# A fused attention and gated-MLP kernel: TensorE's order written out from a clock, head sums over four slices, softmax and weight broadcast in halves

## The chip, the cores and the metric

The kernel runs on one core of one Trainium2 chip, in one launch. The metric is the device time of an execution in microseconds (us). Three runs of the kernel before took 763.28, 763.34 and 765.01 us; their median is 763.34 us.

## The reference

One token sequence of 2048 rows with 1024 features goes through two pre-norm blocks in bf16. The first is a local attention with 32 heads of 32 features. Each position attends to 8 positions, itself and those 2, 4, ... 14 rows back:

```python
qkv = (x @ wqkv).reshape(B, S, 3, H, Dh).transpose(2, 0, 3, 1, 4)
idx = pos[:, None] - (jnp.arange(8) * 2)[None, :]
logits = einsum('bhsd,bhswd->bhsw', q, k[idx]) * Dh ** -0.5     # masked where idx < 0
o = einsum('bhsw,bhswd->bhsd', softmax(logits), v[idx])
h = x + (o heads joined) @ wo                                    # x is layer-normed for wqkv
```

The second is a gated MLP on the layer norm of h. `z = gelu(hn @ w_in)` has 3584 columns. The first half is z1; the second is layer-normed to z2, mixed over the positions (`g = w_sp @ z2 + b_sp`), and the output is `h + (z1 * g) @ w_out`.

## The kernel before, in words

The sequence is cut into four chunks c = 0..3 of 512 rows. The dense work on TensorE (PE) for a chunk is: `qkv(c)` (L225, 192 matmuls of 512 columns), the attention's output projection, called the head, H0 to H3 (`b_head`, L343, 64 matmuls at L358), `b_z2(c)` (L399, 128 matmuls at L415, half of the groups with 256-column tails) and `b_z1(c)` (L439, 112 matmuls at L447). When all chunks are through, the spatial mix (L523) and the output projection (L540) follow; they run with little else beside them.

Each group of 16 matmuls fills one accumulator (`new_acc`, L107), a PSUM tile of two banks out of a ring of three. ScalarE (ACT) empties it: a copy `stg` for qkv (L256), a gelu for z2 and z1 (L417, L450). VectorE (DVE) empties the head's (L369). A fourth pair of banks, tag "L", holds first the logits and then, one after the other, the four tiles `pb` of broadcast weights.

The attention of a chunk (`attention`, L263) is DVE's work with short helpings from PE and ACT. For each of 8 offsets DVE multiplies q and shifted k (L278, 128x4096), adds the upper half of the slices to the lower (L280, 128x2048) and once more (L281, 128x1024). After four offsets PE sums over the features of a head with a 0/1 matrix E32: 8 matmuls with 32 output rows each (L285), placed in four column groups. Then comes the softmax: maximum (L290), subtract (L292), exp on ACT (L296), sum (L298), reciprocal (L300), scale (L302). PE spreads each head's weights over its four partitions (L311) and ACT copies them to AB (L314). Eight products with v and seven additions (L320 to L324) give oT, which the head reads. DVE does the offsets of the next chunk directly after.

Around the head: DVE adds the residual (L369), ACT squares it for the statistics (L371), small DVE steps and one GpSimd (POOL) power give rstd (`batch_rstd`, L327 to L339; the last small step is l2nb at L338), ACT normalizes (`hnc`, L384), and a transposing DMA on SP's queue (L385) makes hnT, the input of z2 and z1. For z2 the chain is the same: ACT squares (L426), the small steps end in l3nb, and DVE normalizes four tiles of 128x1792 (L435). In the last chunk the transposes are made on PE (`head_fin`, L388).

The order on each engine is set by a scheduler from the order of the calls at L461 to L501, from buffer rings and from `tc.high_priority()` blocks; each engine then works strictly in its order and waits where an input or a buffer isn't ready. SP's queue issues most DMAs in order, POOL's queue the loads of q, k, v and of the weights.

Of the kernel before, what the change touches and what calls it, by code (L numbers as in the profile page):

```python
# [10 lines left out]
FP32 = mybir.dt.float32  # L11
BF16 = mybir.dt.bfloat16
# [22 lines left out]
XRB = 2  # L35
# [18 lines left out]
def kernel(  # L54
# [76 lines left out]

    warm = l1.tile([P, CH], BF16, name="warm", tag="xn", bufs=4)
# [91 lines left out]

    def qkv(c):  # L225
# [4 lines left out]
        if c >= 1:  # L230
            xnT[c] = xtp.tile([P, KT, CH], BF16, name="xnT", tag="xnT")
            nc.sync.dma_start_transpose(xnT[c][:], xn_d[c].rearrange("s (a p) -> s a p", p=P))
        for xi in range(3):
            wv = wsb[xi][:].rearrange("p kt (m dl) -> p kt dl m", dl=DLO)
            for dp in range(DLO // 2):
                if c == 0 and xi == 0 and dp < 2:
                    if dp == 0:
                        accs = [new_acc(), new_acc()]
                        for kt in range(KT):
                            for dl in range(4):  # L240
                                T.matmul(accs[dl // 2][:, dl % 2, :], wv[:, kt, dl, :], xnT[c][:, kt, :],  # L241
                                         start=(kt == 0), stop=(kt == KT - 1))
                    acc = accs[dp]
                else:
                    acc = new_acc()
                    for j in range(2):
                        dl = 2 * dp + j
                        for kt in range(KT):
                            T.matmul(acc[:, j, :], wv[:, kt, dl, :], xnT[c][:, kt, :],  # L249
                                     start=(kt == 0), stop=(kt == KT - 1))  # L250
                if c == 0:
                    off = 0 if xi == 0 else HALO
                    A.copy(tiles[xi][:, 2 * dp:2 * dp + 2, off:off + CH], acc[:])  # L253
                else:
                    stg = l1.tile([P, 2, CH], BF16, name="stg", tag="xn", bufs=4)
                    A.copy(stg[:], acc[:])  # L256
                    dma(qkv_d[xi][:, 2 * dp:2 * dp + 2, c * CH:(c + 1) * CH], stg[:])
            if c == 0 and xi > 0:
# [4 lines left out]
    def attention(c):  # L263
        if c == 0:
            qT, kT, vT = att_in[0]
        else:
            qT, kT, vT = alloc_att_in(c)
# [3 lines left out]

        L = ps_att.tile([P, W_WIN, P], FP32, name="L", tag="L")
        for w4 in range(2):
            part = att.tile([P, 4, 2, CH], BF16, name=f"part{w4}", tag="sc8" if w4 == 0 else "part")
            for wi in range(4):
                o = HALO - DIL * (4 * w4 + wi)
                prod = att.tile([P, DLO, CH], BF16, name="prod", tag="prod")
                V.tensor_tensor(prod[:], qT[:], kT[:, :, o:o + CH], op=ALU.mult)  # L278
                t1_ = att.tile([P, 4, CH], BF16, name="t1", tag="t1")
                V.tensor_tensor(t1_[:], prod[:, 0:4, :], prod[:, 4:8, :], op=ALU.add)  # L280
                V.tensor_tensor(part[:, wi], t1_[:, 0:2, :], t1_[:, 2:4, :], op=ALU.add)  # L281
            with tc.high_priority():
                for z in range(2):
                    for sq in range(4):
                        T.matmul(L[32 * sq:32 * sq + 32, 4 * w4:4 * w4 + 4, :], E32, part[:, :, z, sq * P:(sq + 1) * P],  # L285
                                 start=(z == 0), stop=(z == 1), tile_position=(0, 32 * sq))
        if c == 0:
            V.tensor_tensor(L[0:32, :, 0:16], L[0:32, :, 0:16], maskb, op=ALU.add)
        m = att.tile([P, P], FP32, name="mx", tag="mx")
        V.tensor_reduce(m[:], L[:].rearrange("p w s -> p s w"), axis=AX.X, op=ALU.max)  # L290
        Ls = att.tile([P, W_WIN, P], FP32, name="Ls", tag="t1")
        V.tensor_tensor(Ls[:], L[:], m[:].unsqueeze(1).to_broadcast([P, W_WIN, P]), op=ALU.subtract)  # L292
        e_t = att.tile([P, W_WIN, P], BF16, name="e", tag="prod")
        e = e_t[:]
        with tc.high_priority():
            A.activation(e, Ls[:], ACTF.Exp, scale=SCALE)  # L296
        ssum = att.tile([P, P], FP32, name="ssum", tag="ssum")
        V.tensor_reduce(ssum[:], e.rearrange("p w s -> p s w"), axis=AX.X, op=ALU.add)  # L298
        rinv = att.tile([P, P], FP32, name="rinv", tag="rinv")
        V.reciprocal(rinv[:], ssum[:])  # L300
        attn = att.tile([P, W_WIN, P], BF16, name="attn", tag="attn")
        V.tensor_tensor(attn[:], e, rinv[:].unsqueeze(1).to_broadcast([P, W_WIN, P]), op=ALU.mult)  # L302

        AB = att.tile([P, W_WIN, CH], BF16, name="AB", tag="sc8")
        with tc.high_priority():
            for w4 in range(2):
                for sh in range(2):
                    pb = ps_att.tile([P, 2, 4, P], FP32, name="pb", tag="L")
                    for j in range(2):
                        sq = 2 * sh + j  # L310
                        T.matmul(pb[:, j], B4[32 * sq:32 * sq + 32, :],  # L311
                                 attn[32 * sq:32 * sq + 32, 4 * w4:4 * w4 + 4, :],
                                 start=True, stop=True, tile_position=(32 * sq, 0))
                    A.copy(AB[:, 4 * w4:4 * w4 + 4, sh * 256:(sh + 1) * 256].rearrange("p w (j s) -> p j w s", j=2), pb[:])  # L314
        oT = att.tile([P, DLO, CH], BF16, name="oT", tag="oT", bufs=OTB)
        for w in range(W_WIN):
# [4 lines left out]
            else:  # L321
                prod = att.tile([P, DLO, CH], BF16, name="prod", tag="prod")
                V.tensor_tensor(prod[:], vT[:, :, o:o + CH], abb, op=ALU.mult)  # L323
                V.tensor_tensor(oT[:], oT[:], prod[:], op=ALU.add)  # L324
        oTs[c] = oT

    def batch_rstd(sums, sqs, n, pfx):  # L327
# [10 lines left out]
        V.scalar_tensor_tensor(nb[:], mean[:], -1.0, rstd[:], op0=ALU.mult, op1=ALU.mult)  # L338
        return mean, rstd, nb  # L339

    hnTs = {}

    def b_head(c):  # L343
        oT = oTs[c]
        hsum = bp.tile([P, TPC], FP32, name="hsum", tag="hsum")
# [3 lines left out]
        mvl = bp.tile([P, TPC, 2], FP32, name="mvl", tag="mvl", bufs=1)  # L349
        for il in range(TPC):  # L350
# [3 lines left out]
            last = (c == NCH - 1)  # L354
            acc = new_acc()
            for dl in range(DLO):
                for nh in range(2):
                    T.matmul(acc[:, nh, :], oT[:, dl, il * P:(il + 1) * P], wo_sb[:, dl, nh * CH:(nh + 1) * CH],  # L358
                             start=(dl == 0), stop=(dl == DLO - 1))
            accf = acc[:].rearrange("p a b -> p (a b)")  # L360
            hb = bp.tile([P, D], BF16, name="hb", tag="hb", bufs=TPC)
            if last:
                V.tensor_tensor(hb[:], accf, xr[:], op=ALU.add)
                st = bp.tile([P, 2, 6], FP32, name="bnst2", tag="bnst2")
                V.bn_stats(st[:, 0, :], hb[:, 0:512])
                V.bn_stats(st[:, 1, :], hb[:, 512:1024])
                V.bn_aggr(mvl[:, il, :], st[:])
            else:
                V.scalar_tensor_tensor(hb[:], accf, 1.0, xr[:], op0=ALU.mult, op1=ALU.add,  # L369
                                       accum_out=hsum[:, il:il + 1])  # L370
                A.activation(hnc[:, il, :], hb[:], ACTF.Square, accum_out=hsq[:, il:il + 1])  # L371
            dma(h_d[i * P:(i + 1) * P, :], hb[:])
            hbs.append(hb)
        hnT = bp.tile([P, TPC, KT, P], BF16, name="hnT", tag="hnT")
        hnTs[c] = hnT
        if c == NCH - 1:
# [4 lines left out]
            return lambda: head_fin(hnT, hnc, hbs, mvl[:, :, 0], rstdl)  # L381
        mean2, rstd2, nb2 = batch_rstd(hsum[:], hsq[:], D, "l2")
# [5 lines left out]
    def head_fin(hnT, hnc, hbs, mean2, rstd2):  # L388
        for il in range(TPC):
            V.tensor_scalar(hnc[:, il, :], hbs[il][:], mean2[:, il:il + 1], rstd2[:, il:il + 1],  # L390
                            op0=ALU.subtract, op1=ALU.mult)
            tp = ps_tp2.tile([P, KT, P], BF16, name="tp2", tag="tp2")
            for a in range(KT):
                T.transpose(tp[:, a, :], hnc[:, il, a * P:(a + 1) * P], ident)
            V.tensor_copy(hnT[:, il], tp[:])

    z2sb = {}

    def b_z2(c):  # L399
        hnT = hnTs[c]  # L400
# [4 lines left out]
        for il in range(TPC):  # L405
            u = l1.tile([P, FH], BF16, name="u", tag="x4k", bufs=4)
            for hf in range(2):
# [4 lines left out]
                for kt in range(KT):  # L412
                    for n0 in range(0, wd, CH):
                        n1 = min(n0 + CH, wd)
                        T.matmul(accf[:, n0:n1], hnT[:, il, kt, :], wt[:, kt, n0:n1],  # L415
                                 start=(kt == 0), stop=(kt == KT - 1))
                A.activation(u[:, hf * 1024:hf * 1024 + wd], accf[:, 0:wd], ACTF.Gelu_apprx_tanh,  # L417
                             accum_out=sums[:, il, hf:hf + 1])
            if c < NCH - 1:
# [11 lines left out]
        mean3, rstd3, _ = batch_rstd(stot[:], sqs[:], FH, "l3")  # L431
        for il in range(TPC):
            i = c * TPC + il
            z2 = z2t[il]
            V.tensor_scalar(z2[:], us[il][:], mean3[:, il:il + 1], rstd3[:, il:il + 1], op0=ALU.subtract, op1=ALU.mult)  # L435
# [3 lines left out]
    def b_z1(c, lo=0, hi=NF // 2):  # L439
        hnT = hnTs[c]  # L440
        for fp in range(lo, hi):
            acc = new_acc()
            for j in range(2):
                f = 2 * fp + j
                wt, f0 = (wins[2], f) if f < 8 else (wins[3], f - 8)
                for kt in range(KT):
                    T.matmul(acc[:, j, :].rearrange("p (a b) -> p a b", a=TPC), wt[:, kt, f0 * P:(f0 + 1) * P], hnT[:, :, kt, :],  # L447
                             start=(kt == 0), stop=(kt == KT - 1))
            z1s = l1.tile([P, 2, CH], BF16, name="z1s", tag="xn", bufs=4)
            A.activation(z1s[:], acc[:], ACTF.Gelu_apprx_tanh)  # L450
            st = dma(z1_d[2 * fp:2 * fp + 2, :, c * CH:(c + 1) * CH].rearrange("f p s -> p f s"), z1s[:])
        return st
# [7 lines left out]

    qkv(0)  # L461
    qkv(1)
    attention(0)
    qkv(2)
    b_head(0)
    attention(1)
    qkv(3)
# [3 lines left out]
    b_head(1)  # L471
    t1.close()
    t2 = ExitStack()
    bq = t2.enter_context(tc.tile_pool(name="bq", bufs=2))

    for c in range(NCH):
        b_z2(c)
        if c == 0:
            load_win(3, bq.tile([P, KT, 768], BF16, name="win3", bufs=1))
        Z1SPLIT = {1: 0, 2: 3}.get(c, 0)  # L480
        if Z1SPLIT:
            b_z1(c, 0, Z1SPLIT)
        if 0 < c and c + 1 < NCH:
            fin = b_head(c + 1)
        if c + 1 == NCH - 1:
# [7 lines left out]
            ps_tp2 = ctx.enter_context(tc.tile_pool(name="ps_tp2", bufs=2, space=PSUM))  # L493
            fin()
        last_store = b_z1(c, Z1SPLIT)
        if c + 1 == NCH - 1:
            tc.add_manual_dep(wsp0_inst.ins, last_store.ins.name,
                              mybir.DependencyInfo(mybir.DependencyClass.NoSync, mybir.DependencyReason.DATA),
                              reason="keep the xbar transpose out of the z1 store stream")
        if c + 2 < NCH:  # L500
            attention(c + 2)  # L501
# [80 lines left out]
```

## Time and profile before

| what | value |
|---|---|
| median of three runs | 763.34 us |
| the profiled execution's own time | 764.78 us |
| its span, first to last instruction | 763.0 us |
| PE busy | 737.8 us (97%) |
| DVE busy | 440.9 us (58%) |
| ACT busy | 200.0 us (26%) |
| mean granted TensorE clock | 0.987 |
| first spatial matmul (L523) | 468.3 us after the span's start |

How to read it: a profile row has the start and duration in us, engine, line, operation, the tile written and the tiles read. The bracket at its end is the idle time of that engine just before it and who ended it. PE's busy share says little, since a matmul's record lasts about 0.38 us while one starts every 0.216 us; what counts is the distance between starts. Until 468 us, PE's dense work, DVE's attention and ACT's copies go on side by side and wait for each other; after it PE runs 0.216 us per matmul to the end. The change lies entirely in the part before 468 us.

### The profile page before, as it was taken

What the parts mean: (1) busy time and instruction counts of PE and PEld (TensorE: products, weight loads), DVE (VectorE), ACT (ScalarE), POOL (GpSimd) and SP (SyncE); (2) the same over time, 40 slices, a digit from 0 to 9 for tenths busy, and PEclk for the clock granted to TensorE, in tenths of its full rate; (3) what the DMA queues carried; (4) which work ended last, traced back from release to release, by engine and by line L of the source; (5) the groups of instructions that cost most, each with busy time, mean ns of one, the idle gap of its engine ahead of it and who ended that gap; (6) DMA issues with size and microseconds to landing.
All of it is one profiled execution on the core that took longest, in us unless ns stands there. A gap on an engine that the chain in (4) does not pass through costs nothing.

```text
span 763.0 us, 8382 instructions
## 1 busy us (share of the span) xinstructions
PE 737.8 (97%) x3502; PEld 369.5 (48%) x3502; DVE 440.9 (58%) x431; ACT 200.0 (26%) x250; POOL 32.3 (4%) x40
## 2 busy tenths in 40 slices
PE   7999999899998999899989999999999999999997
PEld 3666566455544445344534544444444444444443
DVE  4889799998989799997985010332233122222322
ACT  3332532236318736347611542000000000000000
POOL 0000000010101100000004010000000000000000
PEclk8999999999999999999999999999999999999999
DMA  9994464165893541334057869416211711020001
GB/s 337 335 239 116 142 164 140 55 218 172 233 324 92 172 146 57 125 125 111 0 182 286 209 226 220 161 42 179 70 34 39 191 55 41 28 83 27 1 24 60
DMA packets 109623, 104.20 MB, mean 137 GB/s; under 512 B 63537, under 2 KB 87377, under 8 KB 109457
## 3 DMA queue, kind: packets, MB, share of 16 engines
q1 hardware_dynamic: 103120, 76.89, 33.9%
q0 software_dynamic: 6176, 26.26, 10.1%
q8 instruction: 27, 0.44, 0.3%
q10 hardware_dynamic: 288, 0.52, 0.2%
q14 instruction: 12, 0.09, 0.0%
HBM read 55.09 MB, written 33.88 MB: 117 GB/s over the span
## 4 chain that ended last, share of the span: by engine, by line
PE 60%; DVE 29%; issue 8%; POOL 1%; ACT 1%; DMA 0%; POOLq 0%; DVEq 0%; ACTq 0%
PE acc L523 25%; PE acc L540 12%; DVE oT L324 7%; DVE prod L323 7%; PE acc L249 7%; PE acc L447 6%; DVE prod L278 6%; PE acc L415 3%; PE acc L358 3%; PE acc L241 1%; DVE hb L369 1%; DVE oT L320 1%; PE acc L548 1%; DVE u L435 1%; DMA xp<-in_A_x_dram 0%
## 5 line engine op out<-in xcount | busy, mean ns | idle before, releaser
L278 DVE TENSOR_TENSOR prod<-qT,kT 128x4096 bf16<-128x4096 bf16 x32 | 73.2, 2286 | 2.3 <-ACT kT L253 2.2
L415 PEld LDWEIGHTS <-hnT 128*128 128x128 bf16 x512 | 50.0, 99 | 48.9 <-issue 3.9
L540 PEld LDWEIGHTS <-zg 128*128 128x128 bf16 x420 | 41.1, 98 | 49.5
L323 DVE TENSOR_TENSOR prod<-vT,AB 128x4096 bf16<-128x4096 bf16 x28 | 64.2, 2291 | 1.0
L324 DVE TENSOR_TENSOR oT<-oT,prod 128x4096 bf16<-128x4096 bf16 x28 | 64.2, 2292 | 0.9
L358 PE MATMUL acc<-wo_sb,oT 128*128 128x512 bf16 x256 | 57.6, 387 | 4.8 <-DVE oT L324 4.8
L415 PE MATMUL acc<-win_1620,hnT 128*128 128x512 bf16 x256 | 60.2, 387 | 0.0
L542 DVE TENSOR_TENSOR ot<-acc,hr 128x1024 bf16<-128x1024 f32 x15 | 18.4, 1225 | 69.4 <-PE acc L540 69.4
L249 PE MATMUL acc<-xnT,wv 128*128 128x512 bf16 x256 | 58.3, 386 | 0.0
L447 PE MATMUL acc<-hnT,win_1624 128*128 128x512 bf16 x256 | 58.0, 384 | 0.0
L256 ACT CAST stg<-acc 128x1024 bf16<-128x1024 f32 x36 | 36.2, 1012 | 80.7 <-PE acc L249 70.0
L249 PE MATMUL acc<-xnT,wk 128*128 128x512 bf16 x256 | 56.1, 379 | 0.0
L540 PE MATMUL acc<-wout_a,zg 128*128 128x512 bf16 x240 | 54.2, 379 | 0.0
L249 PE MATMUL acc<-xnT,wq 128*128 128x512 bf16 x224 | 50.3, 381 | 0.0
L450 ACT ACTIVATE z1s<-acc 128x1024 bf16<-128x1024 f32 x28 | 28.6, 1023 | 70.6 <-PE acc L447 69.4
L249 PEld LDWEIGHTS <-wv 128*128 128x128 bf16 x256 | 36.6, 145 | 20.5 <-issue 3.2
L249 PEld LDWEIGHTS <-wk 128*128 128x128 bf16 x256 | 36.8, 144 | 18.7 <-issue 0.4
L415 PE MATMUL acc<-win_1622,hnT 128*128 128x512 bf16 (+1 forms) x256 | 44.4, 326 | 0.0
L358 PEld LDWEIGHTS <-oT 128*128 128x128 bf16 x256 | 25.3, 100 | 36.6 <-DVE oT L324 5.8
L447 PE MATMUL acc<-hnT,win_1922 128*128 128x512 bf16 x192 | 42.8, 379 | 0.0
L540 PE MATMUL acc<-wout_b,zg 128*128 128x512 bf16 x180 | 41.3, 379 | 0.0
L249 PEld LDWEIGHTS <-wq 128*128 128x128 bf16 x224 | 31.8, 145 | 17.0 <-issue 1.8
(358 smaller groups left out, 937.8 us busy)
## 6 DMA issues: line engine op xcount, KB each, us to landing
z_d<-z1s SPq DMA_DIRECT2D x28, 256.0 KB, 2.5
z1c<-z_d SPq DMA_DIRECT2D x28, 256.0 KB, 2.8
z_d<-u SPq DMA_DIRECT2D x12, 448.0 KB, 3.2
xr<-in_A_x_dram SPq DMA_DIRECT2D x16, 256.0 KB, 3.5
h_d<-hb SPq DMA_DIRECT2D x16, 256.0 KB, 3.0
hr<-h_d SPq DMA_DIRECT2D x16, 256.0 KB, 2.8
out_dram<-ot SPq DMA_DIRECT2D x15, 256.0 KB, 2.1
xp<-in_A_x_dram SPq DMA_DIRECT2D x14, 256.0 KB, 10.1
```

Source lines behind the costliest of these rows:

```text
L249: T.matmul(acc[:, j, :], wv[:, kt, dl, :], xnT[c][:, kt, :], start=(kt == 0), stop=(kt == KT - 1))
L256: A.copy(stg[:], acc[:])
L278: V.tensor_tensor(prod[:], qT[:], kT[:, :, o:o + CH], op=ALU.mult)
L323: V.tensor_tensor(prod[:], vT[:, :, o:o + CH], abb, op=ALU.mult)
L324: V.tensor_tensor(oT[:], oT[:], prod[:], op=ALU.add)
L358: T.matmul(acc[:, nh, :], oT[:, dl, il * P:(il + 1) * P], wo_sb[:, dl, nh * CH:(nh + 1) * CH], start=(dl == 0), stop=(dl == DLO - 1))
L415: T.matmul(accf[:, n0:n1], hnT[:, il, kt, :], wt[:, kt, n0:n1], start=(kt == 0), stop=(kt == KT - 1))
L447: T.matmul(acc[:, j, :].rearrange("p (a b) -> p a b", a=TPC), wt[:, kt, f0 * P:(f0 + 1) * P], hnT[:, :, kt, :], start=(kt == 0), stop=(kt ...
L450: A.activation(z1s[:], acc[:], ACTF.Gelu_apprx_tanh)
L523: T.matmul(acc[:, j, :], z2sb[a][:, f * P:(f + 1) * P], wspT[:, a, :], start=(a == 0), stop=(a == NT - 1))
L540: T.matmul(acc[:, nh, :], zg[:, f, il * P:(il + 1) * P], wt[:, f0, nh * CH:(nh + 1) * CH], start=(f == 0), stop=(f == NF - 1))
L542: V.tensor_tensor(ot[:], acc[:].rearrange("p a b -> p (a b)"), hr[:], op=ALU.add)
```

## The change

PE's order is no longer the scheduler's. The scheduler is told to keep PE's program order (`manual_schedule`), and the Python code writes that order out while it emits the kernel. Two counters, `pe_t` and `dve_t`, add up fixed durations. `attention` is a generator that yields the time at which DVE should have the next input for PE ready; before each half tile of dense work `pump` emits the attention pieces that are due by `pe_t`. A head is emitted when its oT should be ready. The other engines are still ordered by the scheduler.

Within the attention the third product step goes (L281): `part` now holds four slices per offset, and PE sums them, for a pair of offsets at a time, with 16 matmuls of 256 columns (four per column group) instead of 8 of 512 per four offsets. Subtract, exp, sum and scale are done in two halves of four offsets, with e kept in fp32. The broadcast is done in halves too, one of the two tiles of a half taken from the accumulator ring. z2 of chunks 0 to 2 is normalized by ACT, with a new instruction per tile, and not by DVE. The residual's buffers go from 2 to 4. H3 still follows three tiles of z1(2). In `head_fin` the four normalizations now stand ahead of the transposes.

The core of the diff:

```diff
-XRB = 2
+XRB = 4
+T_FIRST = 13.0
+SLACK, SLACK3, SLACKB = 3.0, 0.5, 2.0
+H3_AT = 3
+Z2N_ACT = True
...
+    ctx.enter_context(tc.manual_schedule(engines={mybir.EngineType.PE}))
...
+    def did(us): pe_t[0] += us
+    def dve(us): dve_t[0] += us
...
         L = ps_att.tile([P, W_WIN, P], FP32, name="L", tag="L")
-        for w4 in range(2):
-            part = att.tile([P, 4, 2, CH], BF16, ...)
-            for wi in range(4):
...
-                V.tensor_tensor(t1_[:], prod[:, 0:4, :], prod[:, 4:8, :], op=ALU.add)
-                V.tensor_tensor(part[:, wi], t1_[:, 0:2, :], t1_[:, 2:4, :], op=ALU.add)
+        for pr in range(W_WIN // 2):
+            part = att.tile([P, 2, 4, CH], BF16, name="part", tag="part", bufs=2)
+            for wi in range(2):
...
+                V.tensor_tensor(part[:, wi], prod[:, 0:4, :], prod[:, 4:8, :], op=ALU.add)
+                dve(3.42)
+            yield dve_t[0] + (SLACK if pr < 3 else SLACK3)
+            for z in range(4):
+                for sq in range(4):
+                    T.matmul(L[32 * sq:32 * sq + 32, 2 * pr:2 * pr + 2, :], E32, part[:, :, z, sq * P:(sq + 1) * P], ...)
+            did(0.7)
...
+        sme = att.tile([P, 2, W_WIN, P], FP32, name="sme", tag="prod")
+        for hw in range(2):
+            ws = slice(4 * hw, 4 * hw + 4)
+            V.tensor_tensor(sme[:, 0, ws, :], L[:, ws, :], m[:]..., op=ALU.subtract)
+            with tc.high_priority():
+                A.activation(sme[:, 1, ws, :], sme[:, 0, ws, :], ACTF.Exp, scale=SCALE)
+        for hw in range(2):
+            V.tensor_reduce(ssum[:, hw, :], sme[:, 1, 4 * hw:4 * hw + 4, :]..., op=ALU.add)
+        V.tensor_tensor(ssum[:, 0, :], ssum[:, 0, :], ssum[:, 1, :], op=ALU.add)
...
+        for hw in range(2):
+            V.tensor_tensor(attn[:, ws, :], sme[:, 1, ws, :], rinv[:]..., op=ALU.mult)
+            yield dve_t[0] + (0.2 if hw == 0 else SLACKB)
+            for sh in range(2):          # sh 0: tag "L"; sh 1: the accumulator ring
...
+                with tc.high_priority():
+                    A.copy(AB[:, ws, sh * 256:(sh + 1) * 256]..., pb[:])
...
+            if Z2N_ACT and c < NCH - 1:
+                A.activation(z2[:], us[il][:], ACTF.Identity, scale=rstd3[:, il:il + 1], bias=nb3[:, il:il + 1])
+            else:
+                V.tensor_scalar(z2[:], us[il][:], mean3..., rstd3..., op0=ALU.subtract, op1=ALU.mult)
...
+    def pump():
+        while running and min(running.values()) <= pe_t[0]:
+            advance(min(running))
+    def dense(gen, hold=False):
+        for _ in gen:
+            pump()
+            if not hold:
+                c = ready_head()
+                if c is not None and c < NCH - 1:
+                    run_head(c)
...
+    for c in range(NCH):
+        dense(qkv(c), hold=(c == 0))
...
+        dense(b_z2(c))
+        if c == NCH - 2:             # three tiles of z1(2), then H3, then the rest of z1(2)
```

## The prediction

> **What bounds it now.** I read PE's timeline first, then DVE's in the same stretches, then ACT's, then the queue of SP. After 468.3 us PE starts a matmul every 0.216 us to the end, so nothing is to be had there. Before it, PE's timeline shows ten waits for the attention of 0.3 to 3.9 us, 16.8 us in all. Three of them, with the columns start, duration, engine, line, operation, tile, count and idle time before:
>
> ```profile
> 210.36 15.67 PE L358 MATMUL acc<-wo_sb,oT 128*128 128x512 bf16 x64 [2.26 <-DVE oT L324]
> ...
> 324.49 1.05 PE L285 MATMUL L<-part_2620,csb 128*32 128x512 bf16 x8 [3.89 <-DVE part_2620 L281]
> ...
> 390.10 13.99 PE L358 MATMUL acc<-wo_sb,oT 128*128 128x512 bf16 x64 [2.57 <-DVE oT L324]
> ```
>
> The first and the third are the same 64 matmuls. The first took 1.7 us longer: the windows of 25 us there (200 to 250) show a granted clock of 0.93, those around 390 show 1.00. Four such slow starts (143, 210, 235, 324) cost about 1.7 us each. So waits and slow starts take 16.8 + 6.8 = 23.6 us.
>
> DVE is what PE waits for. One offset of the attention:
>
> ```profile
> 49.51 2.29 DVE L278 TENSOR_TENSOR prod<-qT,kT 128x4096 bf16<-128x4096 bf16 x1
> 51.83 1.23 DVE L280 TENSOR_TENSOR t_803<-prod 128x2048 bf16<-128x2048 bf16 x1
> 53.09 0.69 DVE L281 TENSOR_TENSOR part_795<-t_803 128x1024 bf16<-128x1024 bf16 x1
> 53.70 2.28 DVE L278 TENSOR_TENSOR prod<-qT,kT 128x4096 bf16<-128x4096 bf16 x1
> ```
>
> From start to start that is 4.19 us. oT (15 operations) takes 34.85 us, 91.33 to 126.17. The chain: oT(0) ends at 126.2, oT(1) 210.3, oT(2) 301.3, oT(3) 390.0, and H3 starts at 390.1. H3's start sets the end: the same work follows it in both kernels.
>
> ACT has few busy microseconds (26%), but works in order, and some of its pieces are long. The last attention:
>
> ```profile
> 338.65 4.64 ACT L384 ACTIVATE hnc<-hb,l2nb,l2rstd 128x1024 bf16<-128x1024 bf16 x4 [1.22 <-DVE l2nb L338]
> ...
> 345.42 1.28 ACT L296 ACT_TABLE_LOAD   x1
> 346.71 1.06 ACT L296 ACTIVATE e<-Ls 128x1024 bf16<-128x1024 f32 x1
> 347.86 1.28 ACT L450 ACT_TABLE_LOAD   x1
> ...
> 359.97 1.70 ACT L426 ACTIVATE junk<-u 128x1792 bf16<-128x1792 bf16 x1
> ```
>
> Here the normalization of hn was through 2 us before exp was wanted, and z2's normalization was DVE's. And a transposing issue holds SP's queue and the stores behind it:
>
> ```profile
> 181.84 9.32 SPq L385 DMA_TRANSPOSE hnT<-hnc  x1
> 191.21 2.24 SPq L257 DMA_DIRECT2D qkv_d_57<-stg  x2
> ```
>
> **What goes.** Without L281 an offset takes 2.32 + 1.15 = 3.47 us (the add to its next independent start): 0.72 x 32 = 23.0 us less on DVE. z2's normalizing leaves DVE: 2.7 us per chunk. The halves put a few tenths on DVE and let PE start on the first half. I take the chain maximum to first scaled half as 6.3 us (before: 8.1), with a sum half between 0.65 (half of the maximum's 1.23) and 0.98 (half of the sum's 1.95); neither end matters below, where ACT comes last.
>
> **What comes on PE.** 16 helpings of 16 matmuls for 8 of 8. A helping of 8 took 0.6 us in the row at 163.94, its four groups side by side in two steps of 0.22. The new one has four steps of half the columns, so 0.6 again if the groups stay side by side, 16 x 0.108 = 1.7 if not. I take 0.6: 4.8 us more in all; the other end adds 18.
>
> **The walk.** The gain is only what reaches H3, so I followed the changed program's order on each engine, with the durations above. Attention 0 starts at 43.7 as before; its four xn steps (1.9 us) stay in it. Inputs ready 43.7 + 8 x 3.47 + 1.9 = 73.4; PE gets there at 71.8 and waits 1.5. With 11.5 us from there to oT's start (before 12.4 from the same point), oT(0) runs 85.0 to 119.8: 6.4 us earlier.
>
> In attention 1 to 3, l2nb comes after seven offsets, four residual adds and the small steps with POOL's power: 24.3 + 4.6 + 0.8 = 29.7 us after the start. From there ACT's order decides, not DVE's.
>
> Attention 1: l2nb at 149.5; four hnc to 154.2; the transposing issue holds SP (4.9 us in two rows, 9.3 in one beside a 2 MB load; a 1 MB load is beside it here; I take 7) to 161.2. The store of the next stg lands 4.05 us later (195.26 against 191.21 before), and the fourth stg after it waits for that buffer and stands ahead of AB: 165.25. One copy (0.95) and two AB: oT(1) starts at 168.1 and ends at 203.0, 7.3 us earlier than before.
>
> Attention 2: behind the four hnc stand two squares, three gelus, a table load (1.28), the two exps; then a table load, three gelus, a square, two AB. 4.7 + 1.8 + 2.1 + 1.8 + 1.1 + 1.3 + 1.2 + 1.3 + 2.0 + 1.8 + 1.0 + 1.9 = 22.0. So 203.0 + 29.7 + 22.0 + 35.3 (oT with small steps between) = 290.0. 11.3 us earlier.
>
> Attention 3 is the place. DVE's order has the statistics of z2(1) ahead of the maximum. They need the square of its last tile, and that stands on ACT behind the four hnc: 4.7 + 1.0 + 1.8, then the small steps and POOL 1.6: l3nb comes 9.1 us after l2nb, though DVE had its last offset at 3.5. ACT then does three z2 tiles ahead of exp, and one more ahead of the gelu of z1(1)'s second tile. A 128x1792 normalization has no row on ACT; below lies the square's 1.70, above 1.15 x 1792/1024 = 2.0 from hnc. I take 1.9, nearest to the operation of the same kind. 9.1 + 5.6 + 1.3 + 1.2 + 1.9 + 1.3 + 1.0 = 21.4 us after l2nb that gelu frees PE's accumulator; PE has run dry 12.5 after it (last logits at 5.0, then 0.6 and two tiles of 3.45), so it **waits 8.9 us** and starts slowly (8 matmuls in 3.4). Then broadcast and two AB: oT(3) starts at l2nb + 27.4. 290.0 + 29.7 + 27.4 + 34.85 = 382.0: 8.0 us earlier than before.
>
> H3's first accumulator is that of z1(2)'s first tile. Its gelu stands behind four z2 tiles, these behind l3nb, and DVE has these steps behind oT(3): 1.9 + 7.6 + 1.0 = 10.6 us. H3 starts at **392.6**, 2.5 later than before. PE is there at 389.0 (347.1 + 0.4 for the second broadcast, 6.9 z1(1), 24.2 z2(2), 10.4 z1(2)); a wait of 3.6 is in the span of those that ended in a slow start (2.3 to 3.9): 1.7. In `head_fin` the first transpose comes 4.65 us after H3 (before: 404.08 to 408.73); 16 matmuls cover 3.45, where 22 covered 4.75: 1.1 more. Sum 2.5 + 1.7 + 1.1 = **5.3 us**. The rest is as before.
>
> So the profiled execution's own 764.8 becomes 770.1. The median of the runs shown lies 1.4 below that execution, and I put the forecast on it: 763.3 + 5.3 = **768.6**.
>
> **Two rules.** The four slow starts followed idle times of 2.26 to 3.89 us, 2.57 did not bring one. The Trainium skill (TensorE: Matmul & The Clock Gate, What's actually happening) puts the fall to half rate after at least one idle window of about 3.4 us. By it the wait at H3 would stay at full clock or just lose it, and the sum would be some 1.7 lower; the trace decides.
>
> The trace has exp 1.29 us after its table load begins. The skill (ScalarE: Activation LUTs, What ACT_TABLE_LOAD costs) reckons 2.66 us with the drain. By that, two loads in attention 3 would add 2.7 to the sum; the rows say no.
>
> **Rivals.** (a) ACT's order doesn't hold the attention up: the squares and hnc come so early that exp and the gelus wait only for DVE and PE. One point decides: oT(3) must end before about 376, that is l3nb in attention 3 must come some 6 us earlier than I have it. Then PE's floor is 763.3 - 23.6 + 4.8 = 744.5, with a third of the waits left about 752: **faster**. For it: 31 us less on DVE, every head placed by a clock whose constants (3.42, 2.24, 1.73) are close to the rows. Against it: the orders of ACT and DVE are not written out by the change and put hnc, squares and z2 ahead. (b) The column groups of the short matmuls don't run side by side: 18 us more on PE, some of it in time PE waits anyhow: 768.6 + 10 = 779. Against it: weight loads of the four groups start 3 ns apart at 163.94. (c) Gains and stalls cancel: with a 4.9 us transpose, z2 tiles of 1.7 and no slow start at H3 the sum falls by 2.1 + 1.6 + 1.7 to about 763. (d) The clock's sums don't fit and PE waits at places I don't have, above all where it waits for AB to free tag "L" in attention 1: 774.
>
> **Numbers.** Within 0.3% (2.3 us) is about what a measurement can't tell from no change. Forecast with (d) 0.56, (b) 0.06, (c) 0.13, (a) 0.25. So faster 0.25, same 0.13, slower 0.62. The range reaches into (a), to 751, and up to 778, where (b) and the long ends of (d) lie; the forecast's own range is 764 to 774.
>
> **What would show it.** PE idle for 7 to 10 us near 335 to 345 us before an L509 matmul, ended by ACT's z1s. In attention 3, l3nb 8 to 10 us after l2nb. H3 (L400) at 390 to 395 us, waiting for ACT, not for oT. oT(0), oT(1), oT(2) ending near 120, 203, 290. Helpings at L305 of 0.6 us. I am wrong if ACT has its z2 tiles done before DVE's maximum, or if H3 starts before 387.

## The result and the profile after

The changed kernel takes **768.6 us** (median of 4 runs, 767.83 to 770.09). The kernel before, run beside it, takes 764.16 (median of 4, 763.28 to 765.01). The ratio is 1.0061, with a 95% interval of 1.0039 to 1.0082: slower by 4.4 us, though VectorE's (DVE's) busy time fell from 440.9 to 415.7 us. The profiled execution took 767.83 us with a span of 766.1 (before: 764.78 and 763.0).

PE's timeline of the changed kernel, with the columns start, duration, engine, line, operation, tile, count and idle time before with what ended it, at the two places that the prediction named:

```profile
325.03 7.07 PE L509 MATMUL acc<-hnT,win_1852 128*128 128x512 bf16 x32 [0.27 <-ACT u L472]
340.57 3.57 PE L509 MATMUL acc<-hnT,win_1858 128*128 128x512 bf16 x8 [8.47 <-ACT z1s L515]
...
391.99 13.97 PE L400 MATMUL acc<-wo_sb,oT 128*128 128x512 bf16 x64 [2.98 <-ACT z1s L515]
```

The wait at z1(1)'s fifth tile is 8.47 us, and the 8 matmuls after it take 3.57 us where 8 x 0.216 = 1.7 would do: a start at half clock. H3 starts at 391.99 (before: 390.10). It waits for ACT, not for oT. Its 64 matmuls take 13.97 us: here is no slow start.

What ACT did meanwhile, from the same kernel's timeline:

```profile
319.56 4.64 ACT L432 ACTIVATE hnc<-hb,l2nb,l2rstd 128x1024 bf16<-128x1024 bf16 x4 [3.70 <-DVE l2nb L377]
...
326.71 1.00 ACT L515 ACTIVATE z1s<-acc 128x1024 bf16<-128x1024 f32 x1
328.52 5.42 ACT L492 ACTIVATE u<-u,l3nb,l3rstd 128x1792 bf16<-128x1792 bf16 x3 [0.81 <-DVE l3nb L377]
333.96 1.28 ACT L321 ACT_TABLE_LOAD   x1
335.26 1.15 ACT L321 ACTIVATE sme<-sme 128x512 f32<-128x512 f32 x2
336.31 1.87 ACT L492 ACTIVATE u<-u,l3nb,l3rstd 128x1792 bf16<-128x1792 bf16 x1
338.20 1.28 ACT L515 ACT_TABLE_LOAD   x1
339.49 2.86 ACT L515 ACTIVATE z1s<-acc 128x1024 bf16<-128x1024 f32 x3
...
383.84 7.20 ACT L492 ACTIVATE u<-u,l3nb,l3rstd 128x1792 bf16<-128x1792 bf16 x4 [2.42 <-DVE l3nb L377]
390.94 2.81 ACT L515 ACTIVATE z1s<-acc 128x1024 bf16<-128x1024 f32 x3
```

And the two small steps of VectorE that ACT waits for there:

```profile
319.36 0.16 DVE L377 SCALAR_TENSOR_TENSOR l2nb<-l2mean,l2rstd 128x4 f32<-128x4 f32 x1 [0.92 <-POOL l2rstd L375]
...
328.32 0.17 DVE L377 SCALAR_TENSOR_TENSOR l3nb<-l3mean,l3rstd 128x4 f32<-128x4 f32 x1 [1.12 <-POOL l3rstd L375]
```

Read ACT's lines backwards. PE's fifth tile needs the accumulator that the gelu at 339.49 empties. Ahead of that gelu stand a table load, a z2 tile, two exps, another load and three z2 tiles. The first of these could not begin before l3nb, 8.96 us after l2nb. The same happens at H3: four z2 tiles (7.20 us) stand ahead of the gelu that frees its first accumulator.

One offset of the attention, which lost its second add, on VectorE:

```profile
46.54 2.29 DVE L299 TENSOR_TENSOR prod<-qT,kT 128x4096 bf16<-128x4096 bf16 x1
48.87 1.23 DVE L300 TENSOR_TENSOR part<-prod 128x2048 bf16<-128x2048 bf16 x1
50.13 2.29 DVE L299 TENSOR_TENSOR prod<-qT,kT 128x4096 bf16<-128x4096 bf16 x1
```

From start to start that is 3.59 us (before: 4.19). The ends of oT were 118.4, 202.0, 289.2 and 381.5 (before: 126.1, 210.3, 301.3, 390.0). So the last attention did end 8.5 us earlier, and H3 could not use it.

### The profile page after: what moved, and what is told of

The parts are those of the page before. It is cut to its first block, busy times and chain, and to the rows that moved or that the text cites. A ratio compares the mean times of both kernels' runs of the same rounds, so it can differ in the third digit from the quotient of the medians.

```text
span 766.1 us, 8760 instructions
## 1 busy us (share of the span) xinstructions
PE 735.6 (96%) x3694; PEld 371.9 (49%) x3694; DVE 415.7 (54%) x403; ACT 219.6 (29%) x266; POOL 34.5 (5%) x40
## 3 DMA queue, kind: packets, MB, share of 16 engines
q0 software_dynamic: 6176, 26.26, 10.2%
## 4 chain that ended last, share of the span: by engine, by line
PE 64%; DVE 22%; issue 7%; ACT 4%; POOL 2%; DMA 1%; POOLq 0%; DVEq 0%; ACTq 0%
PE acc L637 25%; PE acc L263 12%; PE acc L654 12%; DVE oT L362 6%; DVE prod L361 6%; PE acc L509 5%; DVE prod L299 5%; PE acc L400 4%; PE acc L469 3%; DVE part L300 2%; ACT u L492 1%; DVE hb L413 1%; PE acc L254 1%; ACT hnc L432 1%; PE acc L662 1%
## 5 line engine op out<-in xcount | busy, mean ns | idle before, releaser
L469 PE MATMUL acc<-win_1848,hnT 128*128 128x512 bf16 x256 | 57.9, 379 | 0.0
L263 PEld LDWEIGHTS <-wk 128*128 128x128 bf16 x256 | 36.6, 144 | 18.7 <-issue 0.9
L654 PE MATMUL acc<-wout_b,zg 128*128 128x512 bf16 x180 | 41.3, 379 | 0.0
```

The costliest lines, as they stand in the source:

```text
L263: T.matmul(acc[:, j, :], wv[:, kt, dl, :], xnT[c][:, kt, :], start=(kt == 0), stop=(kt == KT - 1))
L654: T.matmul(acc[:, nh, :], zg[:, f, il * P:(il + 1) * P], wt[:, f0, nh * CH:(nh + 1) * CH], start=(f == 0), stop=(f == NF - 1))
```

## The experiments

Twelve kernels, each timed in turns with the kernel before. H3 is its start in the profiled execution, and the last column is PE's longest wait between 45 and 405 us there.

| kernel | median us | ratio to before, 95% interval | H3 | longest PE wait, ended by |
|---|---|---|---|---|
| changed kernel | 768.6 | 1.0061 (1.0039 to 1.0082) | 392.0 | 8.47, ACT gelu |
| e1_att3_order | 761.09 | 0.9956 (0.9939 to 0.9974) | 381.6 | 4.14, ACT gelu |
| e2_h3_order | 765.51 | 1.0007 (0.9990 to 1.0025) | 390.9 | 8.47, ACT gelu |
| e3_both_orders | 754.52 | 0.9873 (0.9846 to 0.9900) | 378.6 | 2.22, ACT gelu |
| e4_z2_on_vectore | 759.11 | 0.9930 (0.9905 to 0.9954) | 384.8 | 4.36, DVE oT |
| e5_add_back | 786.86 | 1.0293 (1.0265 to 1.0322) | 407.5 | 15.47, DVE oT |
| e6_before_pairs | 770.68 | 1.0085 (1.0060 to 1.0111) | 398.2 | 3.07, DVE part |
| e7_planner_order | 768.59 | 1.0043 (1.0026 to 1.0059) | 391.4 | 7.89, DVE attn |
| e8_hn_late | 755.52 | 0.9884 (0.9859 to 0.9909) | 380.0 | 7.80, ACT gelu |
| e9_z2_0_late | 749.40 | 0.9806 (0.9793 to 0.9820) | 371.4 | 1.99, DVE part |
| e10_help_twice | 761.89 | 0.9965 (0.9950 to 0.9979) | 386.1 | 3.18, ACT gelu |
| e11_order_only | 783.18 | 1.0248 (1.0231 to 1.0264) | 405.3 | 17.73, DVE oT |
| e12_before_z2_act | 767.69 | 1.0038 (1.0020 to 1.0055) | 391.7 | 2.91, DVE part |

**Theory 1** is the prediction's: the order of ACT's queue (and of VectorE's small steps ahead of it) holds attention 3 and H3. **Theory 2**: the changed kernel pays for its short matmuls and its PE order, and the long wait only stands where PE would wait anyhow. **Theory 3**: VectorE's work is still the bound.

### e1, e2, e3: only queues change

The edit keeps PE's order, instruction by instruction. `behind(a, b)` is a scheduling dependency that puts a behind b in the order without a semaphore. In b_z2 the statistics and z2's tiles of chunk 1 (e1), of chunk 2 (e2) or of both (e3) are put into `fin_z2`, called later:

```diff
+        def fin_z2(stat_after=None, z2_after=None):
...
+                with tc.high_priority():
+                    behind(V.tensor_tensor(stot[:], sums[:, :, 0], sums[:, :, 1], op=ALU.add), stat_after)
+                    mean3, rstd3, nb3 = batch_rstd(stot[:], sqs[:], FH, "l3")
...
+                    behind(A.activation(z2[:], us[il][:], ACTF.Identity, scale=rstd3[:, il:il + 1], bias=nb3[:, il:il + 1]), z2_after)
...
             run_head(NCH - 1)
+            if c in LATE:
+                z2_fin.pop()(None, z1_gelu[0])
...
             dense(b_z1(c))
+            if c in LATE:
...
+                z2_fin.pop()(att_last[0], ab_last[0])
```

The first call is that of chunk 2, the second that of chunk 1. `att_last` is the second scaled half of attention 3, `ab_last` its last AB, `z1_gelu` the gelu of z1(2)'s last tile ahead of H3.

Expected of e1:

> The changed kernel with one thing moved: the l3 statistics of z2(1) stand behind attention 3's second scaled half on VectorE, and its four z2 tiles behind the last AB on ACT. PE's order is the same, instruction by instruction. Theory 1 (ACT's and VectorE's queue orders hold attention 3 up): exp of attention 3 about 5 us earlier (330 for 335), the 8.5 us wait of PE at z1(1) gone, oT(3) starts at 338 to 341 for 346.7, H3 starts at oT(3)'s end plus the 10 us of l3 small steps and z2 tiles, 384 to 386 for 392, time 768.6 - 7 = 761 to 762. Theory 2 (the changed kernel is slower for what its short matmuls and its written PE order cost; the 8.5 us only stand where PE would wait anyhow, later): H3 moves by less than 1.5 us, time 767 to 769. Theory 3 (VectorE's work is the bound): oT(3) moves by less than 2 us.

Measured: 761.09, H3 at 381.64, oT(3) from 336.3 (changed kernel: 346.7). The wait at z1(1) is gone. oT(3) and H3 came some 2 us earlier than I had put them, but H3 waits 4.14 us for ACT's gelu behind the z2 tiles and then starts slowly: 16.39 us for its 64 matmuls.

Expected of e2:

> The changed kernel with only the four z2 tiles of chunk 2 moved behind the gelus of z1(2)'s three tiles ahead of H3 on ACT (nothing else differs on any engine). Theory 1: the 3.0 us wait at H3 goes, H3 at 389, time 765.6 (765 to 766.5). Theory 2: another wait takes its place (oT(3) or an xr load), time 768 to 769.

Measured: 765.51; H3 follows the matmul before it without a wait. That is 3.1 us less than the changed kernel.

Expected of e3:

> Both moves together. Theory 1: PE's wait at z1(1) and the one at H3 both gone, H3 at PE's own arrival, about 379 to 381, for oT(3) ends near 374: 768.6 - 11 = 757 to 759, faster than both kernels. Theory 2: 766 to 769. Theory 3: H3 not before 388, time over 765.

Measured: 754.52, below the 757 to 759 I expected, faster than both kernels, and 14.1 us less than the changed kernel, which is more than 7.5 + 3.1: with attention 3 early the wait at H3 had grown, and it went too. ACT and PE in this kernel's timelines:

```profile
326.68 1.92 ACT L536 ACTIVATE z1s<-acc 128x1024 bf16<-128x1024 f32 x2
328.61 1.28 ACT L323 ACT_TABLE_LOAD   x1
329.90 1.15 ACT L323 ACTIVATE sme<-sme 128x512 f32<-128x512 f32 x2
...
339.68 3.67 ACT L507 ACTIVATE u<-u,l3nb,l3rstd 128x1792 bf16<-128x1792 bf16 x2
```

```profile
325.00 8.79 PE L530 MATMUL acc<-hnT,win 128*128 128x512 bf16 x40 [0.27 <-ACT u L481]
334.65 0.39 PE L347 MATMUL pb<-attn,csb 32*128 32x512 bf16 x2 [0.86 <-DVE attn L334]
...
378.63 13.98 PE L402 MATMUL acc<-wo_sb,oT 128*128 128x512 bf16 x64
```

The first two gelus now stand ahead of the exps, and the z2 tiles come after the last copies to AB (337.89 and 338.78). PE runs 40 matmuls where it ran 32 and stopped for 8.47 us, and H3 has no idle time before it. No instruction was removed, so theories 2 and 3 fall: the short matmuls and VectorE's operations are the same.

### e4: z2 back on VectorE

```diff
-Z2N_ACT = True
+Z2N_ACT = False
```

> The changed kernel with z2's normalization back on VectorE in all chunks (PE's order the same). VectorE gets 2.7 us per chunk more, in attention 3 ahead of the maximum (its queue has statistics, four tiles, maximum). Theory 1: ACT has exp and gelus free, the 8.5 us wait at z1(1) goes and H3 waits for oT(3) alone: H3 at 381 to 385, time 758 to 762, so moving z2 to ACT was the loss. Theory 2: 768 to 770. Theory 3 (VectorE is the bound): oT(3) ends 3 to 5 us later, time 772 to 774.

Measured: 759.11, H3 at 384.8. VectorE's timeline shows what is remarkable here:

```profile
331.35 0.16 DVE L377 SCALAR_TENSOR_TENSOR l3nb<-l3mean,l3rstd 128x4 f32<-128x4 f32 x1 [1.12 <-POOL l3rstd L375]
331.43 2.71 DVE L494 TENSOR_SCALAR u<-u,l3mean,l3rstd 128x1792 bf16<-128x1792 bf16 x4
334.06 1.22 DVE L313 TENSOR_REDUCE mx<-L 128x128 f32<-128x1024 f32 x1
```

The maximum starts at 334.06, later than in the changed kernel (328.40) by 5.7 us, or 4.7 counted from the attention's start, and the kernel is 9.5 us faster. So the late maximum is not what cost. ACT, free of z2, does two gelus while it waits for the exp (in its timeline at 329.74 and 330.93), and PE has no wait at z1(1). A z2 tile is 0.68 us on VectorE and 1.8 on ACT. The price on VectorE shows too: oT(2) ends 2.6 us later than in the changed kernel, counted from the same start, and PE waits 4.36 us for it.

### e5, e6, e11, e12: each part alone, or left out

e5 is the changed kernel with the add back (helpings of 8 of 256 columns, the clock at 4.14):

```diff
+                V.tensor_tensor(prod[:, 0:4, :], prod[:, 0:4, :], prod[:, 4:8, :], op=ALU.add)
-                V.tensor_tensor(part[:, wi], prod[:, 0:4, :], prod[:, 4:8, :], op=ALU.add)
+                V.tensor_tensor(part[:, wi], prod[:, 0:2, :], prod[:, 2:4, :], op=ALU.add)
...
-            for z in range(4):
+            for z in range(2):
```

> The changed kernel with the second add back on VectorE: two slices per offset, helpings of 8 matmuls of 256 columns for 16, the order's clock at 4.14 us per offset for 3.42. VectorE gets 0.7 us per offset more, 23 us in all; PE gets at most 16 x 0.3 = 5 us back. Theory 1 (the attention sets H3, and the saving on VectorE is real, spent again by ACT's order in attention 3): oT ends 6, 12, 17, 20 us later, H3 at 400 or later, time 775 to 783. Theory 2 (the helpings are the loss): 763 to 766.

Measured: 786.86, beyond the upper end. oT ended at 125.5, 214.3, 311.3 and 407.5: 7, 12, 22 and 26 us later, and H3 waited 15.47 us for it. So the saved add, with the clock that goes with it, is worth 18.3 us in the changed kernel. Not all of that is VectorE's longer work: in attention 3 its maximum waits 6.97 us for PE's last helping. What the smaller helpings gave back is not separated.

e6 is the kernel before with the pairs and the four slices alone:

```diff
-        for w4 in range(2):
+        for pr in range(4):
...
-                V.tensor_tensor(t1_[:], prod[:, 0:4, :], prod[:, 4:8, :], op=ALU.add)
-                V.tensor_tensor(part[:, wi], t1_[:, 0:2, :], t1_[:, 2:4, :], op=ALU.add)
+                V.tensor_tensor(part[:, wi], prod[:, 0:4, :], prod[:, 4:8, :], op=ALU.add)
```

> The kernel before with one part of the change alone: no second add, four slices per pair of offsets, helpings of 16 matmuls of 256 columns. PE's order is the planner's, softmax whole, z2 on VectorE. Theory 1: VectorE's 23 us reach PE through the old queues (no z2 tiles on ACT): the 23.6 us of waits and slow starts shrink by a half to three quarters, 4.8 us of helpings come: 763.5 - 15 + 4.8 = 753 (748 to 758). Theory 2 (the helpings eat what the add saves): 763 to 769.

Measured: 770.68. My expectation of 753 fell, and theory 2's number is nearer, but not for its reason. Three of the fifteen waits of 0.35 us and more in PE's timeline:

```profile
211.02 0.62 PE L283 MATMUL L<-part,csb 128*32 128x256 bf16 x16 [3.07 <-DVE part L279]
...
240.23 0.62 PE L283 MATMUL L<-part,csb 128*32 128x256 bf16 x16 [3.00 <-DVE part L279]
...
340.48 0.39 PE L309 MATMUL pb<-attn,csb 32*128 32x512 bf16 x2 [2.25 <-DVE attn L300]
```

The fifteen sum to 18.7 us (kernel before: ten, 16.8), and four slow starts follow, as before. By the pages PE is busy 5.9 us longer (743.7 for 737.8), most of it in eight more helpings, and idle 2.2 us longer: the 8.1 us between the two spans. oT(3) ended 9 us earlier than before, but H3 started 8 us later, without a wait of its own. So VectorE did give its time back, and the planner moved the helpings forward with it: the last one of attention 3 stands behind 1325 long matmuls, where it stood behind 1453, and PE waits again. In this kernel where a helping stands in PE's order took back what VectorE had won.

e11 is the changed kernel without the saving and with z2 on VectorE (the edits of e4 and e5 together): the written order and the halves alone.

> The changed kernel without its two other parts: the second add back on VectorE (helpings of 8 of 256, clock 4.14) and z2's normalization back on VectorE, so the order written from the clock and the halves alone. With the kernel before (764.6), e6_before_pairs (770.7: the saving alone) and e4_z2_on_vectore (759.1: both) it fills the table of two by two. Theory 1 (order and saving only pay together: the order leaves room where the logits come, and VectorE must be fast enough to use it): VectorE's chain is what H3 waits for, 4 x 5.8 us later than e4, so 768 to 778. Rival (the order and the halves are the gain by themselves): 755 to 760.

Measured: 783.18, worse than I gave either. H3 waits 17.73 us for oT(3). Much of the excess is in attention 3: from oT(2)'s end to oT(3)'s end it takes 100.1 us for 85.2 in e4, of which the eight adds explain 5.8. There the maximum waits 6.16 us for PE's last helping, and PE had waited 3.31 us for hnT ahead of it (346.53). How the rest comes about I did not take apart.

e12 is the kernel before with z2's tiles of chunks 0 to 2 on ACT:

```diff
+            if c < NCH - 1:
+                A.activation(z2[:], us[il][:], ACTF.Identity, scale=rstd3[:, il:il + 1], bias=nb3[:, il:il + 1])
+            else:
-            V.tensor_scalar(z2[:], us[il][:], mean3[:, il:il + 1], rstd3[:, il:il + 1], op0=ALU.subtract, op1=ALU.mult)
+                V.tensor_scalar(z2[:], us[il][:], mean3[:, il:il + 1], rstd3[:, il:il + 1], op0=ALU.subtract, op1=ALU.mult)
```

> The kernel before with the third part of the change alone: z2's normalization of chunks 0 to 2 on ACT (1.8 us a tile) for VectorE (0.65). The planner orders all engines. Theory 1 (what counts is which short-lived work of ACT the tiles stand ahead of): in its queue the four tiles of chunk 1 stand between squares, those of chunk 2 behind two gelus of z1(2) and ahead of the third, so only VectorE's 2.7 us per chunk is won and a wait of 1 to 4 us at H3 may come: 763 to 768. Rival (moving z2 off VectorE is a gain by itself, VectorE being what PE waits for): 757 to 761.

Measured: 767.69. A wait of 2.72 us for a gelu is new in chunk 0, and H3 starts at 391.66 for 390.10.

So every part alone makes the old kernel slower (6, 19 and 3 us), and only the saving and the order together make it faster (e4: 0.9930). They need each other: that much the runs show. The reading that goes with it is that the order takes the helpings away from where PE would wait, and that the saving lets VectorE keep up with that order; in e5 and e11 the order itself also fits VectorE badly, since the maximum waits for PE. The order was not run without the halves, the four residual buffers and the new order in `head_fin`, so "order" stands for these too.

### e7: the planner orders PE

```diff
-    ctx.enter_context(tc.manual_schedule(engines={mybir.EngineType.PE}))
```

> The changed kernel without its written order on PE: the planner places PE's instructions too, all else as changed. Theory 1 (the queues of ACT and VectorE in attention 3 decide, whoever orders PE): 763 to 772, with a wait of PE for ACT in attention 3 still there. Rival (the written order, whose clock says 3.42 for the 3.59 of the trace and knows nothing of ACT, is what costs): 752 to 758.

Measured: 768.59, the changed kernel's time, with a wait of 7.89 us at the same place, ended by the scaled half that the late exp brings. It undoes less than I had meant: the planner mostly follows the order in which the clock emits. In attention 3 it moves one pair of broadcast matmuls eight places forward and another one place back, and in `head_fin` it puts 22 matmuls of z1(2) ahead of the first transpose again, where the changed kernel has 16. So it shows only that holding the planner to this order matters little for the time.

### e8, e9: the same rule at the next places

e3 still has waits of 1.54 us (154.35, for stg) and 2.22 us (239.76, for u), each with a slow start. e8 puts hnc's tiles and the transposing issue of chunks 0 and 1 behind the last AB of the next attention:

```diff
+        def norm(first=None):
+            for il in range(TPC):
+                behind(A.activation(hnc[:, il, :], hbs[il][:], ACTF.Identity, scale=rstd2[:, il:il + 1], bias=nb2[:, il:il + 1]), first)
...
         oT = att.tile([P, DLO, CH], BF16, name="oT", tag="oT", bufs=OTB)
+        while norms:
+            norms.pop()(ab_last[0])
```

> Run e3_both_orders with one thing more: the four hnc tiles and the transposing issue of chunks 0 and 1 stand behind the last AB of attention 1 and 2 on ACT and SP (chunk 2 as before). PE's order is the same. Theory 1 (hnc and the transposing issue ahead of gelus, stores and copies make PE's waits of 1.7 us at 152.5 and 2.4 us at 237.3, each with a slow start of 1.7): both go, 754.5 - 5 to 7 = 748 to 750. Theory 2 (PE would wait for the logits or hnT there anyhow): 753 to 756.

Measured: 755.52, no gain. Both waits are gone as theory 1 said, and in their place stands one of 7.80 us. ACT's timeline shows why:

```profile
250.00 4.67 ACT L437 ACTIVATE hnc<-hb,l2nb,l2rstd 128x1024 bf16<-128x1024 bf16 x4
254.68 7.20 ACT L514 ACTIVATE u<-u,l3nb,l3rstd 128x1792 bf16<-128x1792 bf16 x4
261.79 2.81 ACT L543 ACTIVATE z1s<-acc 128x1024 bf16<-128x1024 f32 x3
```

Eight long tiles, 11.9 us, now stand in a row ahead of z1(0)'s first gelu. e9 puts chunk 0's z2 tiles behind the fourth gelu of z1(0), by `fin_z2` as in e1.

> Run e8_hn_late with the four z2 tiles of chunk 0 behind the first four gelus of z1(0) on ACT, where e8 had them, behind the four hnc tiles, ahead of the first gelu. PE's order is the same. Theory 1 (in e8 the wait at hnc only moved into the 7.8 us wait at 262.8, eight tiles of 1.2 and 1.8 us in a row ahead of a gelu): that wait goes, no PE wait over 2 us is left, 755.5 - 8 = 747 (746 to 749). Theory 2 (the wait moves on once more, to hnT(1) or to u's buffers): 752 to 756.

Measured: **749.40**, ratio 0.9806 (0.9793 to 0.9820), the fastest here. The clock stays at full rate from 4.35 to 745.05 us and H3 starts at 371.41. It is 2.4 us over the 747 I expected: two of its five executions lie in my range (747.24, the profiled one, and 747.87), three at 749.4 to 749.6.

### e10: the price of a helping

```diff
+            for _ in range(2):
                 for z in range(4):
```

This is e3 with every helping issued twice; the second writes the same sums again.

> Run e3_both_orders with every helping of 16 short matmuls issued twice over (the second writes the same sums again), 256 more matmuls of 256 columns on PE. It prices a helping where PE is the bound. If the four column groups run side by side and all of it lies on PE's path: 16 x 0.62 = 9.9 us more, 764.4 (763 to 766). If the groups run one after another: 16 x 1.73 = 28 us more, 782. If the helpings hide in PE's waits: under 4 us, 755 to 758.

Measured: 761.89, 7.4 us over e3, between two of my three cases. PE's timeline of e10:

```profile
59.68 1.06 PE L308 MATMUL L<-part,csb 128*32 128x256 bf16 x32
60.67 7.13 PE L264 MATMUL acc<-xnT,wq 128*128 128x512 bf16 x31
```

32 matmuls take 1.06 us where 16 took 0.62: the second 16 cost 0.44, four steps of 0.108, so the four groups run side by side. 16 x 0.44 = 7.0. I had priced the added ones like helpings that stand alone. From the last long matmul ahead to the first behind, a helping without a wait takes PE 0.65 us more in the changed kernel.

## Why the prediction was right

**What bounds it.** That the same work follows H3 held: from H3 to the span's end are 372.9 us before, 374.1 after, 374.1 in e3 and 374.1 in e9. The 1.2 is the shorter cover at the transposes, taken as 1.1: e7, with 22 matmuls there again, has 373.0.

**The saving.** An offset is 3.59 us, not 3.47. The next product writes the same `prod` buffer that the add reads, so it is not the independent start I took. That is 1 us in oT(0), and in attention 1 to 3 l2nb comes 30.2 us after the end of the oT before it, for the 29.7 I had.

**The helpings.** 0.62 each, as taken; on PE eight more of them are 8 x 0.65 = 5.2, for 4.8.

**The walk.** The profiled execution began its attention at 41.37 us for 43.74; in the kernel before the clock was at half rate from 10.12 to 16.95, in the changed one it was not. Counted from the same start, oT ended 0.9, 1.4, 1.6 and 1.9 us later than I had it. From l2nb to oT's start I had 18.6, 22.0 and 27.4 us in attention 1, 2 and 3; measured were 18.7, 21.2 and 27.3. l3nb came 8.96 us after l2nb (9.1), the z2 tile took 1.8 (1.9), PE waited 8.47 (8.9). e1 and e4 show that this chain held attention 3 up: without it oT(3) starts, counted from the same start, 10.7 us earlier in e1 and 4.4 in e4.

**The sum.** The 5.3 us held H3's shift of 2.5, a slow start of 1.7 and 1.1 at the transposes. The step that failed is the slow start of 1.7 us: the wait at H3 was 2.98 us for 3.6, and no slow start followed. I had taken it from the length of the wait alone; the runs show that it also matters where the wait falls on the clock's steps (last section). In the place of the 1.7 the walk was 1.8 us later from the same start. So the profiled kernel stands 766.1 - 763.0 + 2.4 = 5.5 us over the one before, and two errors of the same size cancel. Of the medians, the base was 764.16 with the new runs, not 763.3, and the difference 4.4. That the forecast meets the median to a tenth is partly luck.

**The two rules.** The Trainium skill (TensorE: Matmul & The Clock Gate, What's actually happening) has the rate fall after an idle window of about 3.4 us. Read as an idle time of that length, it keeps the wait of 2.98 us at H3 at full clock, as measured, but would keep the waits of 1.54 and 2.22 us in e3 there too, and these ended in half clock. The measurement decides: in these runs less than a whole idle step was enough (last section). Its 2.66 us for a table load (ScalarE: Activation LUTs, What ACT_TABLE_LOAD costs) is not seen: exp starts 1.30 us after the load begins (333.96 to 335.26).

**The rivals.** (a) fell: ACT's order did hold the attention up. Its point of decision and its price hold in e3, where oT(3) ends at 372.4, before 376, and the time is 754.5 for the 752 I gave it. (b) fell by e10. Of (c)'s three gains one came, the missing slow start at H3; a z2 tile took 1.8 us and the transposing issue of attention 1 held SP's queue for 6.31 us, not 4.9. Of (d), waits at 154.4 and 239.8 that I had not listed did come, for stg and u. What they cost in the changed kernel no run shows, since none takes them out there alone; e9, where they are gone, is 5.1 us faster than e3.

## What to carry to other kernels

When work is moved to an engine that looks idle, ask what stands behind it in that engine's queue: four tiles of 1.8 us ahead of a gelu that frees an accumulator, at two places, cost 14 us, more than the change had won, and putting them (and the small steps before them) later took no instruction away. A faster producer gains only if the consumer's order leaves room for it, so change both together and look again, since the wait moves to the next long row of the queue. It is found by following the waiting instruction's releaser backwards in its engine's queue, not by the busy share (ACT's was under 30% throughout).

## What the runs showed of the hardware that I had not expected

- A slow start does not go by the length of the idle time alone. Half clock followed waits of 2.22 and 1.54 us (e3, at 239.8 and 154.4) and 4.14 (e1); it did not follow 2.98 (changed kernel) or 2.57 (kernel before). What sorts them is a grid in time: within each of the fourteen profiled executions, all changes of the granted clock lie whole steps of 3.413 us apart, over the whole span. Count for each step the time in which no matmul record runs. Between 45 and 745 us the clock fell 38 times, always at the end of a step with 1.80 us or more of it. Every step at full clock with more than 2.0 us ended so; of the ten with 1.80 to 2.0 us four did. The 2.98 us at H3 cross the end of a step at 390.21, so that 1.20 us fell into one step and 1.78 into the next. The same two waits, 0.49 us ahead of a helping and 1.55 behind it, put 2.04 us into one step in the changed kernel (first line) and 1.76 in e1 (second line), and the same 32 matmuls take 8.76 us there and 7.07 here:

```profile
154.38 8.76 PE L263 MATMUL acc<-xnT,wv 128*128 128x512 bf16 x32 [1.55 <-ACT stg L273]
...
154.76 7.07 PE L264 MATMUL acc<-xnT,wv 128*128 128x512 bf16 x32 [1.55 <-ACT stg L274]
```

- Executions differ in their first microseconds. Where PE has no half-rate record there, the attention starts at 41.3 to 41.8 us (changed kernel, e1, e3, e7, e9), with one of 3.4 us at 42.1 to 42.4 (e4, e5, e8, e10), with 6.8 us at 43.7 to 44.0 (kernel before, e2, e6, e12), with 10.2 us at 44.9 (e11). All that follows moves with it: up to there e2 has the instructions of the changed kernel in the same order, and its profiled execution starts the attention 2.3 us later.
